# An early start, dummy matmuls, 64-column tiles and crossbar transposes in a fused attention and token-mixing kernel

## Chip, cores, metric

One core of one Trainium2 chip. The metric is the device time of one execution in microseconds (us). A run counts as slow when it is over 1.5% above the fastest of the same kernel; comparisons use the other (fast) runs. The profiler's span is some 1.8 us shorter than the time of the same run.

## The reference, cut to what matters

```python
# x: 8 x 8 x 512 x 64 (batch, head, token, d), state: 8 x 8 x 32 x 64
a     = softmax(x @ state.T / 8);  xread = a @ state      # 512 tokens read 32 slots
a2    = softmax(state @ x.T / 8);  sread = a2 @ x         # 32 slots read 512 tokens
y     = concat([xread, sread], tokens)                    # 8 x 544 x 512 (heads side by side)
mixed = ((y @ w_q) @ (y @ w_k).T / 8) @ y                 # no softmax: V = (y@w_k).T @ y is 64 x 512
out   = relu(mixed) @ w_out
```

## The kernel before

Per batch, with the names that the profile shows: `xT` transposes x on TensorE, `pt` forms the scores, `exp` their exponentials E, `rs`/`rinv`/`A` normalise on VectorE and GpSimd, `at` transposes A, `srd` and `sums` form the second read and its divisors, `wq`, `wk`, `g`, `v` build the 64 x 512 matrix V, `mix` applies it, `fin` multiplies by w_out (the largest item). The order of all steps on all engines is one list, ORDER; an entry is step, batch, engine (t TensorE, v VectorE, a ScalarE, p GpSimd). Each engine executes its entries in order. TensorE is PE below, VectorE DVE, ScalarE ACT, GpSimd POOL, the queue that issues loads and stores SP. A matmul is a weight load, which puts one operand into the array (the stationary one), and the matmul itself, which moves the other operand through it.

```python
nc.sync.dma_start(out=st_f, in_=state.rearrange("b h n d -> (b h) (n d)")...)   # all state, 512 KB, first
for g in range(4):                                     # x of batch 0, four transfers
    eng = nc.sync if g % 2 == 0 else nc.scalar
    eng.dma_start(out=x_f0[:, 2*g:2*g+2], in_=xsrc(0, 2*g, 2*g+2))
# ... 16 warm-up matmuls on zeros ...
def xT_mm(n, b, e):                                    # transposes on TensorE
    for q in range(NP):
        for u in range(2):
            nc.tensor.transpose(out=ps[:, u, q, :],
                in_=x_bf[b][:, NP*r+q, 128*u:128*u+128], identity=ident)
def pt_mm(n, b, e):                                    # 8 matmuls, 64 columns moved
    for u in range(2):
        for q in range(NP):
            nc.tensor.matmul(out=ps[:, 2*u:2*u+2, NS*q:NS*q+NS],
                lhsT=L[b][f"xTe{r}"][:, u, q, :], rhs=stT[:, b, :, NP*r+q, :], ...)
def fin_acc(ps, lhs):                                  # 4 matmuls, 512 columns moved
    for k in range(KC):
        nc.tensor.matmul(out=ps, lhsT=lhs(k), rhs=w_o[:, k, :], start=(k==0), stop=(k==KC-1))
# ... the other steps; loads of batches 1 to 7 on POOL ...
for tok in ORDER.split(): ...
```

The softmax here doesn't subtract the row's maximum and nothing guards it: scores larger than these inputs give would overflow.

## Time and profile before

| | before |
|---|---|
| median time | 96.12 us (95.58 to 96.66, 3 runs); 95.4 to 96.3 in later calls |
| span, profiled run | 93.4 us |
| busy: PE, DVE, ACT, POOL | 79.8, 56.2, 53.6, 44.6 us |
| instructions in PE's stream (two for each matmul) | 2,754 |
| first `mix` of batch 0; last matmul ends | 27.5 us; 87.75 us |

The prediction below shows the lines on which it rests. One view that it only quotes in words is this: busy time of each engine in a stretch (us busy and number of instructions; then the granted PE clock, the DMA share and GB/s; the DMA share is the time of all packets over that of 16 engines, and can go above 1, since packets' times can overlap), here from the first `mix` to the last matmul of the kernel before.

```profile
27.50:87.80 60.30, 59.07 (x908) 36.89 (x907) 40.15 (x71) 36.06 (x56) 26.43 (x30) 1.00 0.48 147
```

PE is busy for 59.07 of 60.30 us at full clock. That leaves 1.23 us.

### The profile page before, as it was taken

What the parts mean: (1) busy time and instruction counts of PE and PEld (TensorE: products, weight loads), DVE (VectorE), ACT (ScalarE), POOL (GpSimd) and SP (SyncE); (2) the same over time, 40 slices, a digit from 0 to 9 for tenths busy, and PEclk for the clock granted to TensorE, in tenths of its full rate; (3) what the DMA queues carried; (4) which work ended last, traced back from release to release, by engine and by line L of the source; (5) the groups of instructions that cost most, each with busy time, mean ns of one, the idle gap of its engine ahead of it and who ended that gap; (6) DMA issues with size and microseconds to landing.
All of it is one profiled execution on the core that took longest, in us unless ns stands there. A gap on an engine that the chain in (4) does not pass through costs nothing.

```text
span 93.4 us, 3134 instructions
## 1 busy us (share of the span) xinstructions
PE 79.8 (85%) x1376; PEld 53.4 (57%) x1376; DVE 56.2 (60%) x109; ACT 53.6 (57%) x80; POOL 44.6 (48%) x58
## 2 busy tenths in 40 slices
PE   5908098998995999999999999999999999999500
PEld 3506086896864676888366547646668644444100
DVE  1026948589584959896496198965786487222500
ACT  2324746687894687359967647864054876444200
POOL 7307994894499989899500009339750000000000
PEclk9998555599999999999999999999999999999985
DMA  1998799999999915500032517806455004428990
GB/s 28 305 260 193 94 160 156 205 203 194 197 199 197 201 18 232 225 11 0 0 130 102 225 22 213 311 30 270 186 225 232 0 0 164 173 39 300 400 363 21
DMA packets 12933, 15.13 MB, mean 162 GB/s; under 512 B 1592, under 2 KB 10296, under 8 KB 12856
## 3 DMA queue, kind: packets, MB, share of 16 engines
q0 software_dynamic: 7808, 4.19, 33.2%
q1 hardware_dynamic: 4280, 9.70, 29.3%
q10 hardware_dynamic: 832, 1.05, 3.8%
q8 instruction: 10, 0.16, 0.7%
q14 instruction: 3, 0.02, 0.1%
HBM read 10.22 MB, written 8.91 MB: 205 GB/s over the span
## 4 chain that ended last, share of the span: by engine, by line
PE 76%; ACT 6%; DMA 6%; DVE 4%; issue 2%; DVEq 0%
PE fin_ps L538 30%; PE xT_ps L246 9%; DMA st_f<-in_state_dram 6%; PE pt_ps L264 5%; PE mix_ps L504 5%; PE at_ps L322 4%; PE srd_ps L335 3%; PE wq_ps L398 3%; PE wk_ps L436 3%; DVE stT L139 3%; ACT xT L137 2%; PE fins_ps L538 2%; PE srd_ps L348 2%; PE v_ps L468 2%; PE g_ps L452 2%
## 5 line engine op out<-in xcount | busy, mean ns | idle before, releaser
L538 PE MATMUL fin_ps<-w_o,rmix 128*128 128x512 bf16 x128 | 30.0, 379 | 0.0
L309 POOL TENSOR_TENSOR A<-E,rinv 128x1024 bf16<-128x1024 bf16 (+1 forms) x9 | 15.3, 1718 | 15.5 <-DVE rinv L303 15.5
L538 PEld LDWEIGHTS <-rmix 128*128 128x128 bf16 x128 | 11.6, 98 | 12.5 <-ACT rmix L143 0.3
L137 ACT COPY ost<-fin_ps 128x1024 f32<-128x1024 f32 (+1 forms) x10 | 9.3, 928 | 14.1 <-PE fin_ps L538 13.6
L139 DVE COPY ost<-fin_ps 128x1024 f32<-128x1024 f32 (+1 forms) x8 | 8.7, 1089 | 11.1 <-PE fin_ps L538 7.5
L280 ACT ACTIVATE E<-pt_ps 128x512 bf16<-128x512 f32 x16 | 9.6, 603 | 4.3 <-PE pt_ps L264 4.3
L372 POOL TENSOR_TENSOR sbd<-srn,mask 128x256 bf16<-128x256 bf16 x16 | 9.5, 612 | 4.4 <-DVE srn L362 4.1
L295 DVE TENSOR_REDUCE rsum<-E 128x16 f32<-128x512 bf16 x16 | 10.6, 672 | 1.1 <-ACT E L280 1.1
L246 PE MATMUL xT_ps<-ident,x_bf 128*128 128x128 bf16 x128 | 11.0, 238 | 0.1
L145 DVE TENSOR_SCALAR rmix<-mix_ps 128x1024 bf16<-128x1024 f32 x7 | 8.5, 1223 | 2.7 <-PE mix_ps L504 2.6
L137 ACT COPY xT<-xT_ps 128x1024 bf16<-128x1024 bf16 x9 | 9.1, 1020 | 1.5 <-PE xT_ps L246 1.5
L143 ACT ACTIVATE rmix<-mix_ps 128x1024 bf16<-128x1024 f32 x9 | 9.3, 1032 | 0.7 <-PE mix_ps L504 0.5
L213 POOL TENSOR_TENSOR stbd<-st_bf,mask 128x256 bf16<-128x256 bf16 x16 | 9.3, 614 | 0.0
L246 PEld LDWEIGHTS <-x_bf 128*128 128x128 bf16 x128 | 8.4, 106 | 1.0 <-issue 0.4
L264 PE MATMUL pt_ps<-stT,xT 128*128 128x64 bf16 x128 | 7.1, 203 | 0.5 <-DVE xT L139 0.4
L504 PE MATMUL mix_ps<-wq,V 64*128 64x256 bf16 x64 | 5.7, 272 | 1.2 <-issue 1.1
...
L264 PEld LDWEIGHTS <-xT 128*128 128x128 bf16 x128 | 5.6, 105 | 1.6 <-DVE xT L139 0.5
L139 DVE COPY xT<-xT_ps 128x1024 bf16<-128x1024 bf16 x7 | 4.8, 686 | 2.2 <-PE xT_ps L246 2.0
L139 DVE COPY AT<-at_ps 128x1024 bf16<-128x1024 bf16 x7 | 4.8, 685 | 1.2 <-PE at_ps L322 1.2
L322 PE MATMUL at_ps<-ident,A 128*128 128x128 bf16 x64 | 5.0, 219 | 0.0
L504 PEld LDWEIGHTS <-V 64*128 64x128 bf16 x64 | 2.4, 94 | 3.8 <-issue 2.8
...
## 6 DMA issues: line engine op xcount, KB each, us to landing
...
```

The source lines that it names most:

```text
L137: nc.scalar.copy(out=out, in_=in_)
L139: nc.vector.tensor_copy(out=out, in_=in_)
L143: nc.scalar.activation(out=out, in_=in_, func=AF.Relu)
L213: nc.gpsimd.tensor_tensor(out=stbd[:, b, r], in0=st_bf[:, b, r : r + 1, :].to_broadcast((128, NP, D)), in1=mask[:, :, None].to_broadcast(( ...
L246: nc.tensor.transpose(out=ps[:, u, q, :], in_=x_bf[b][:, NP * r + q, 128 * u : 128 * u + 128], identity=ident,)
L264: nc.tensor.matmul(out=ps[:, 2 * u : 2 * u + 2, NS * q : NS * q + NS], lhsT=L[b][f"xTe{r}"][:, u, q, :], rhs=stT[:, b, :, NP * r + q, :], ...
L280: nc.scalar.activation(out=L[b]["E"][:, r].rearrange("p c q n -> p c (q n)"), in_=L[b][f"pt{r}"], func=AF.Exp, scale=float(scale),)
L295: nc.vector.reduce_sum(out=L[b]["rsum"][:, w], in_=L[b]["E"].rearrange("p r c q n -> p (r c q) n")[:, w], axis=AX.X,)
L309: eng.tensor_tensor(out=L[b]["A"].rearrange("p r c q n -> p (r c q) n")[:, w], in0=L[b]["E"].rearrange("p r c q n -> p (r c q) n")[:, w], ...
L372: nc.gpsimd.tensor_tensor(out=L[b]["sbd"][:, r], in0=L[b]["srn"][:, r : r + 1, :].to_broadcast((128, NP, D)), in1=mask[:, :, None].to_broa ...
L504: nc.tensor.matmul(out=ps[:, h, kk, :], lhsT=L[b]["V"][rows, 128 * k : 128 * k + 128], rhs=L[b]["wq"][rows, 0:SH], start=True, stop=True,)
L538: nc.tensor.matmul(out=ps, lhsT=lhs(k), rhs=w_o[:, k, :], start=(k == 0), stop=(k == KC - 1))
```

## The change

Five things, and a rewritten ORDER. The state is loaded with heads in rows and batch 0's part first, so that the transposes back go. Batch 1's x is asked for earlier. `fill` entries put 52 dummy matmuls on zeros into PE's waits, to keep its clock up. Entries marked `c` cut a matmul with 128 stationary columns into two with 64, meant to spare PE the change of tiling between neighbours. `xs` transposes x of batches 5 to 7 by a DMA through the crossbar.

```diff
-    nc.sync.dma_start(out=st_f, in_=state... # 512 KB)
+    def st_load(b0, b1):
+        nc.sync.dma_start(out=st_f[:, b0:b1], in_=st_src[:, 2 * b0 : 2 * b1])
+    st_load(0, 1)              # then x of batch 0, then st_load(1, 3); st_load(3, 8) behind a gate on POOL
+    def fill(n, b, e):
+        ps = psA.tile([128, 256], FP, name="fill_ps", tag="psA")
+        for w in range(b):
+            nc.tensor.matmul(out=ps, lhsT=zero[:, 0:128], rhs=zero, start=True, stop=True)
+    def mm(m, out, lhsT, rhs, **kw):
+        if m == "c":
+            for h in range(2):
+                lh = ... lhsT[:, 64 * h : 64 * h + 64]
+                nc.tensor.matmul(out=out[64 * h : 64 * h + 64], lhsT=lh, rhs=rhs, **kw)
+        else:
+            nc.tensor.matmul(out=out, lhsT=lhsT, rhs=rhs, **kw)
     def pt_mm(n, b, e):        # likewise xT, at, srT, wk, g, sums, fin, fs
-                nc.tensor.matmul(
+                mm(e,
+    def x_dT(n, b, e):
+        xT = work.tile([128, H, 2, 128], BF, name="xTd", bufs=3)
+        nc.sync.dma_start(out=xT..., in_=x_bf[b]..., transpose=True)
-    stb (state transposed back) and its copy, st_in (cast of the whole state)
 ORDER: rewritten; stores of fin are now entries of their own (os); the last tile is copied by halves
```

More of the change, by code (lines that the diff above doesn't have):

```diff
@@ L16 @@
 ORDER = """
-zst.0.p stc0.0.v stc1.0.a stt0.0.t xc0.0.p stt1.0.t xc1.0.a ste0.0.v ix1.0.p stf0.0.a xT0.0.t
-stf1.0.v ix2.0.p ste1.0.a iwo.0.p xc2.0.v stb.0.t xc3.0.v ix3.0.p xTe0.0.v stbe.0.a xT1.0.t wc.0.p
-pt0.0.t xTe1.0.v exp0.0.a pt1.0.t ix4.0.p rs0.0.v sw.0.t exp1.0.a sw.1.t rinv0.0.v xT0.1.t swe.0.a
-ix5.0.p rs1.0.v srd.0.t xTe0.1.a sums.0.t rinv1.0.v ix6.0.p sw.2.t srn.0.v xT1.1.t swe.2.a swe.1.v
-pt0.1.t A1.0.p srT.0.t xT1.2.t exp0.1.a srTe.0.v xTe1.1.v xT0.2.t xTe1.2.a A0.0.p at1.0.t rs0.1.v
@@ L22 @@
-pt1.1.t sw.3.t exp1.1.a xTe0.2.v pt1.2.t ix7.0.p at0.0.t swe.3.a srd.1.t ate.0.v pt0.2.t exp1.2.a
-stbd.0.p sums.1.t rs1.1.v wq.0.t exp0.2.a wks.0.t srn.1.v wk.0.t wqe.0.a sbd.0.p srd.2.t rinv.1.v
-wke.0.a srT.1.t xT1.3.t rs0.2.v srTe.1.a g.0.t sbd.1.p sums.2.t xTe1.3.a xT0.3.t ge.0.v srn.2.v
-v.0.t rs1.2.v xTe0.3.a sbd.2.p pt1.3.t srT.2.t srTe.2.v exp1.3.a ve.0.v pt0.3.t stbd.1.p xT1.4.t
-exp0.3.a rinv.2.v mixs.0.t mix0.0.t xTe1.4.v mse.0.a mix1.0.t A.2.p mxe0.0.a srd.3.t mxe1.0.v
-pt1.4.t sums.3.t xT1.5.t exp1.4.a xT0.4.t xTe1.5.v fin0.0.t A.1.p xTe0.4.a srn.3.v fin1.0.t rs1.3.v
@@ L28 @@
-rs0.3.v srT.3.t fin2.0.t sbd.3.p srTe.3.a rinv.3.v oe0.0.a at.1.t rs1.4.v pt0.4.t A.3.p at.2.t
-ate.1.a fin3.0.t ate.2.v exp0.4.a wq.1.t oe1.0.v wks.1.t stbd.2.p wqe.1.a wk.1.t srd.4.t wke.1.a
-wq.2.t rs0.4.v stbd.4.p wks.2.t g.1.t wqe.2.v wk.2.t sums.4.t wke.2.a ge.1.v at.3.t stbd.3.p srn.4.v
-g.2.t ate.3.v srT.4.t ge.2.a v.1.t srTe.4.a sbd.4.p rinv.4.v v.2.t ve.1.v wq.3.t ve.2.a wks.3.t
-wk.3.t wqe.3.v A.4.p mix0.1.t wke.3.v mixs.2.t mix1.1.t mxe0.1.a mixs.1.t mse.2.v pt1.5.t g.3.t
-mse.1.v xT1.6.t exp1.5.a stbd.6.p mix1.2.t xTe1.6.v xT0.7.t mxe1.1.a at.4.t rs1.5.v stbd.5.p pt1.6.t
@@ L34 @@
-ge.3.a fin2.1.t ate.4.v mxe1.2.a fin3.1.t stbd.7.p exp1.6.a mix0.2.t xTe0.7.a oe1.1.v v.3.t wq.4.t
-mxe0.2.a wks.4.t wqe.4.v pt0.7.t fin0.1.t ve.3.v exp0.7.a fin1.1.t rs1.6.v rs0.7.v mix0.3.t oe0.1.a
-mixs.3.t wk.4.t mse.3.v xT1.7.t wke.4.v fs.3.t mxe0.3.a fin2.2.t xTe1.7.a fin3.2.t fse.3.a g.4.t
-oe1.2.v pt1.7.t fin0.2.t exp1.7.a fin1.2.t ge.4.v rs1.7.v mix1.3.t oe0.2.a rinv.7.v v.4.t mxe1.3.v
-A.7.p srd.7.t ve.4.a sums.7.t xT0.6.t srn.7.v mix0.4.t xTe0.6.a mix1.4.t mxe0.4.v mixs.4.t sbd.7.p
-srT.7.t at.7.t mse.4.a pt0.6.t xT0.5.t exp0.6.a mxe1.4.v fin2.3.t xTe0.5.a fin3.3.t srTe.7.v ate.7.v
@@ L40 @@
-pt0.5.t oe1.3.a fin0.4.t rs0.6.v rinv.6.v fin1.4.t exp0.5.a A.6.p rs0.5.v srd.6.t oe0.4.a srd.5.t
-sums.5.t rinv.5.v fin0.3.t srn.5.v A.5.p fin1.3.t at.6.t oe0.3.v srT.5.t sums.6.t fin2.4.t sbd.5.p
-ate.6.v at.5.t fin3.4.t srTe.5.v srn.6.v wq.7.t ate.5.v oe1.4.a sbd.6.p wks.7.t srT.6.t wk.7.t
-wqe.7.v wq.5.t srTe.6.a wke.7.v wks.5.t wk.5.t wqe.5.v g.7.t wq.6.t wke.5.v ge.7.a wks.6.t wqe.6.a
-wk.6.t g.5.t wke.6.a v.7.t ge.5.v v.5.t ve.7.a g.6.t ve.5.a mix1.7.t ge.6.v mix0.7.t mxe1.7.a
-mixs.7.t v.6.t mxe0.7.v mixs.5.t mix1.5.t mse.5.a ve.6.a mse.7.v mix0.5.t fin2.7.1 mxe0.5.v mxe1.5.a
@@ L46 @@
-fin3.7.1 oc2.7.v mix0.6.t oc3.7.a mix1.6.t mixs.6.t fin1.7.1 mxe1.6.v mse.6.a mxe0.6.a fs.7.t
-oc1.7.v fin2.6.t fse.7.a fin3.6.t fin2.5.t oe1.6.a fin3.5.t fin0.5.t oe1.5.v fin1.5.t fin0.6.t
-oe0.5.a fin1.6.t fin0.7.1 oe0.6.v oc0.7.a
+zst.0.p ix1.0.p stc.0.v fill.2.t stt.0.c ste.0.a stbd.0.p stf.0.a xc1.0.a xc0.0.p xc2.0.v ix2.0.p
+fill.21.t xT0.0.c xc3.0.v xTe0.0.v fill.2.t xT1.0.c iwo.0.p stc.1.v fill.2.t pt0.0.c ix3.0.p
+xTe1.0.v fill.2.t stt.1.c exp0.0.a stf.1.v fill.2.t pt1.0.c ste.1.a ix4.0.p rs0.0.v exp1.0.a
@@ new lines @@
+rinv0.0.v stbd.2.p wc.0.a fill.9.t sums.0.c rs1.0.v fill.2.t srd.0.r fill.2.t xT0.1.t srn.0.v A0.0.p
+rinv1.0.v fill.2.t sw.0.r xTe0.1.v fill.2.t srT.0.c xT1.1.c A1.0.p at0.0.c srTe.0.v xTe1.1.a pt0.1.c
+swe.0.v stg.0.p at1.0.c ix5.0.p exp0.1.a pt1.1.c ate.0.v exp1.1.a xT0.2.c ix6.0.p rs0.1.v wq.0.c
+xTe0.2.a wks.0.c wk.0.c wqe.0.v xT1.2.c sbd.0.p rs1.1.v sums.1.c wke.0.a srd.1.r rinv.1.v g.0.c
+stbd.1.p pt0.2.c srn.1.v ge.0.a xTe1.2.v exp0.2.a fill.1.t v.0.c srT.1.c sbd.1.p ve.0.a pt1.2.c
+srTe.1.v rs0.2.v exp1.2.a fill.3.t mix0.0.r A.1.p mixs.0.r stc.2.v mix1.0.r mxe0.0.a sums.2.t
@@ new lines @@
+mxe1.0.v srd.2.r xT1.3.c mse.0.a stt.3.c xTe1.3.a stt.2.c rs1.2.v stbd.3.p fin2.0.c rinv.2.v stf.2.a
+stf.3.v xT0.4.c stbd.7.p ste.3.v xT1.4.c xTe0.4.a ste.2.v at.1.c fin3.0.c stbd.5.p ate.1.v xTe1.4.a
+pt1.3.c srn.2.v sw.1.r stbd.4.p oe1.0.a srT.2.c swe.1.v xT0.3.c wq.1.c xTe0.3.v A.2.p exp1.3.a
+os1.0.s sw.2.r sw.3.r swe.2.a rs1.3.v pt0.3.c wks.1.c wk.1.c exp0.3.a fin0.0.c wke.1.v stbd.6.p
+srTe.2.a rs0.3.v at.2.c swe.3.a pt0.4.c rinv.3.v fin1.0.c wqe.1.a sbd.2.p ate.2.v exp0.4.a g.1.c
+xs.5.s pt1.4.c oe0.0.a rs0.4.v sums.3.c A.3.p srd.3.r ge.1.v wq.2.c exp1.4.a srn.3.v wks.2.c wk.2.c
@@ new lines @@
+wqe.2.v srT.3.c wke.2.a v.1.c rs1.4.v sbd.3.p srTe.3.a at.3.c ve.1.a g.2.c ate.3.v sums.4.c srd.4.r
+ix7.0.p xs.6.s mixs.1.r ge.2.v mix1.1.r mse.1.a mix0.1.r srn.4.v mxe1.1.a v.2.c rinv.4.v sbd.4.p
+srT.4.c wq.3.c ve.2.v wks.3.c wk.3.c mxe0.1.a wqe.3.v pt1.5.c A.4.p mix0.2.r wke.3.v pt0.5.c
+exp1.5.a fin2.1.c srTe.4.v exp0.5.a rs1.5.v xs.7.s g.3.c mxe0.2.a fin3.1.c ge.3.v rs0.5.v v.3.c
+oe1.1.a rinv.5.v at.4.c ve.3.v A.5.p sums.5.c srd.5.r ate.4.v mix1.2.r mixs.3.r mix0.3.r mxe1.2.a
+os1.1.s mse.3.v pt0.6.c wq.4.c srn.5.v wks.4.c os0.0.s wk.4.c exp0.6.a wqe.4.v sbd.5.p srT.5.c
@@ new lines @@
+fin2.2.c srTe.5.v mxe0.3.a wke.4.v fin3.2.c rs0.6.v pt1.7.c oe1.2.a mix1.3.r pt0.7.c mxe1.3.v at.5.c
+exp0.7.a pt1.6.c os1.2.s fin0.1.c exp1.6.a ate.5.v fin2.3.c exp1.7.a rs0.7.v wq.5.c rs1.7.v wks.5.c
+fin3.3.c wqe.5.a rinv.7.v rs1.6.v A.7.p sums.6.c sums.7.c oe1.3.a srd.7.r rinv.6.v srd.6.r srn.7.v
+wk.5.c fin1.1.c os1.3.s srn.6.v wke.5.a A.6.p srT.7.c g.5.c srTe.7.v at.7.c ge.5.v fin0.3.c ate.7.v
+fin1.3.c sbd.6.p oe0.1.v at.6.c oe0.3.a sbd.7.p wq.7.c os0.1.s ate.6.v wks.7.c wk.7.c srT.6.c
+fin0.2.c wqe.7.v os0.3.s wke.7.a srTe.6.a g.7.c fin1.2.c ge.7.v v.7.c oe0.2.v wq.6.c ve.7.a wks.6.c
@@ new lines @@
+wk.6.c mixs.2.r wqe.6.a mix1.7.r os0.2.s mse.2.v mix0.7.r mxe1.7.a mixs.7.r wke.6.v g.4.c v.5.c
+ge.4.v g.6.c mse.7.v ve.5.a v.4.c ge.6.v fs.3.c mxe0.7.a ve.4.v mix1.5.r fse.3.v mixs.4.r mix1.4.r
+mxe1.5.a v.6.c mxe1.4.v fix1.7.c ve.6.a mix0.4.r mse.4.v oc1.7.a mixs.6.r mix1.6.r mxe0.4.v fix0.7.t
+mxe1.6.a mixs.5.r mix0.6.r mse.6.a mse.5.v mix0.5.r oc0.7.a mxe0.6.v fix2.7.t fs.7.t oc2.7.a
+mxe0.5.v fin0.6.t fse.7.v fin1.6.t fin0.4.t oe0.6.v fin1.4.t os0.6.s fin2.6.t oe0.4.v fin3.6.t
+os0.4.s fin2.4.t oe1.6.a fin3.4.t os1.6.s fin0.5.t oe1.4.v fin1.5.t os1.4.s fin2.5.t oe0.5.v
@@ L49 @@
+fin3.5.t os0.5.s fix3.7.t oe1.5.v oc3.7.b os1.5.s
 """
@@ L80 @@
     work = ctx.enter_context(tc.tile_pool(name="work", bufs=4))
-    tail = ctx.enter_context(tc.tile_pool(name="tail", bufs=6))
+    tail = ctx.enter_context(tc.tile_pool(name="tail", bufs=5))
     psA = ctx.enter_context(tc.tile_pool(name="psA", bufs=2, space=bass.MemoryType.PSUM))
@@ L85 @@
     x_bf = [const.tile([128, H, NC * D], BF, name=f"x_bf{b}") for b in range(B)]
-    st_f = const.tile([B * H, NS, D], FP, name="st_f")
-    st_in = const.tile([B * H, NS, D], BF, name="st_in")
+    st_f = const.tile([128, B, 2, D], FP, name="st_f")
     x_f0 = const.tile([128, H, NC * D], FP, name="x_f0")
@@ L100 @@
     zero = const.tile([128, 256], BF, name="zero")
+    gate = st_f[:, 3, 0, 0:1]
     rmix_s = const.tile([128, 2, KC, 4, NS], BF, name="rmix_s")
@@ L105, in xsrc @@
         return x[b, h0:h1].rearrange("h (p c) d -> p h (c d)", c=NC)
+    st_src = state.rearrange("b (r q) n d -> (q n) (b r) d", r=2)
     wsrc = [w.rearrange("(r q d) j -> r d q j", r=2, q=NP) for w in (moe_w_q, moe_w_k)]
     dst_x = out[:, 0:S].rearrange("b (p c) e -> b p c e", c=NC)
-    nc.sync.dma_start(
-        out=st_f, in_=state.rearrange("b h n d -> (b h) (n d)").rearrange("p (n d) -> p n d", n=NS)
-    )
+    def st_load(b0, b1):
+        nc.sync.dma_start(out=st_f[:, b0:b1], in_=st_src[:, 2 * b0 : 2 * b1])
+    st_load(0, 1)
     for g in range(4):
@@ L115 @@
         eng.dma_start(out=x_f0[:, 2 * g : 2 * g + 2], in_=xsrc(0, 2 * g, 2 * g + 2))
+    st_load(1, 3)
     for t in range(2):
@@ L145, in relu, with tr @@
             nc.vector.tensor_scalar(out=out, in0=in_, scalar1=0.0, scalar2=None, op0=ALU.max)
+    def fill(n, b, e):
[5 more added lines that the diff above has]
+            for h in range(2):
+                lh = lhsT[:, 2 * h : 2 * h + 2, :] if len(lhsT.shape) == 3 else lhsT[:, 64 * h : 64 * h + 64]
+                nc.tensor.matmul(out=out[64 * h : 64 * h + 64], lhsT=lh, rhs=rhs, **kw)
+        else:
+            nc.tensor.matmul(out=out, lhsT=lhsT, rhs=rhs, **kw)
+    def tr(m, out, in_):
+        for h in range(2):
+            w = slice(64 * h, 64 * h + 64)
+            if m == "c":
+                i = in_[:, 2 * h : 2 * h + 2, :] if len(in_.shape) == 3 else in_[:, w]
+                nc.tensor.transpose(out=out[w], in_=i, identity=ident)
+            elif m == "r":
+                nc.tensor.transpose(out=out[:, w], in_=in_[w], identity=ident[w, w])
+            elif h == 0:
+                nc.tensor.transpose(out=out, in_=in_, identity=ident)
     def load(n, b, e):
@@ L160, in x_cast, with st_gate, st_cast @@
             copy(e, o, i)
-    def st_cast(n, b, e):
-        w = slice(16 * int(n[-1]), 16 * int(n[-1]) + 16)
-        copy(e, st_in[:, w], st_f[:, w])
+    def st_gate(n, b, e):
+        nc.gpsimd.memset(gate, 0.0)
+        st_load(3, B)
+    SC = [(0, 1), (1, 3), (3, B)]
+    SG = [(0, 1), (1, 3), (3, 6), (6, B)]
+    def st_cast(n, g, e):
+        b0, b1 = SC[g]
+        copy(e, st_bf[:, b0:b1], st_f[:, b0:b1])
     def zeros(n, b, e):
@@ L173, in w_cast, with st_tr, st_ev @@
             copy(e, w_qk, w_f)
-    def st_tr(n, b, e):
-        g = int(n[-1])
-        ps = psB.tile([128, NS // 2, B * H], BF, name="stT_ps", tag="psB")
-        for m in range(NS // 2):
-            for c2 in range(2):
-                nc.tensor.transpose(
-                    out=ps[64 * c2 : 64 * c2 + 64, m, :],
-                    in_=st_in[:, g * (NS // 2) + m, :],
-                    identity=ident[0:64, 0:64],
-                )
+    def st_tr(n, g, e):
+        b0, b1 = SG[g]
+        ps = psB.tile([128, b1 - b0, 2, HN], BF, name="stT_ps", tag="psB")
+        for b in range(b0, b1):
+            for r in range(2):
+                for c2 in range(2):
+                    nc.tensor.transpose(
+                        out=ps[64 * c2 : 64 * c2 + 64, b - b0, r, :],
+                        in_=st_bf[:, b, r, :],
+                        identity=ident,
+                    )
         G[g] = ps
-    def st_ev(n, b, e):
-        g = int(n[-1])
-        c2 = 0 if n[:3] == "ste" else 1
+    def st_ev(n, g, e):
+        b0, b1 = SG[g]
+        c2 = 0 if n == "ste" else 1
         rows = slice(64 * c2, 64 * c2 + 64)
@@ L192, in st_ev @@
             e,
-            stT[rows, :, c2, :, g * (NS // 2) : (g + 1) * (NS // 2)],
-            G[g][rows].rearrange("p n (b h) -> p b h n", b=B),
-        )
-    def st_back(n, b, e):
-        ps = psB.tile([128, B, 2, D], BF, name="stb_ps", tag="psB")
-        for b in range(B):
-            for r in range(2):
-                nc.tensor.transpose(
-                    out=ps[:, b, r, :],
-                    in_=stT[0:64, b, 0, NP * r : NP * r + NP, :],
-                    identity=ident[0:64, 0:64],
-                )
-        G["stb"] = ps
-    def stb_ev(n, b, e):
-        copy(e, st_bf, G["stb"])
+            stT[rows, b0:b1, c2].rearrange("p b h n -> p b (h n)"),
+            G[g][rows].rearrange("p b r m -> p b (r m)"),
+        )
     def stbd_blk(n, b, e):
@@ L245, in xT_mm @@
             for u in range(2):
-                nc.tensor.transpose(
-                    out=ps[:, u, q, :],
-                    in_=x_bf[b][:, NP * r + q, 128 * u : 128 * u + 128],
-                    identity=ident,
-                )
+                tr(e, ps[:, u, q, :], x_bf[b][:, NP * r + q, 128 * u : 128 * u + 128])
         L[b][n] = ps
@@ L254, in xT_ev, with a_dT @@
         r = int(n[-1])
-        xT = work.tile([128, 2, NP, 128], BF, name=f"xT{r}")
+        xT = work.tile([128, 2, NP, 128], BF, name=f"xT{r}", bufs=3)
         copy(e, xT, L[b][f"xT{r}"])
         L[b][n] = xT
+    def x_dT(n, b, e):
+        xT = work.tile([128, H, 2, 128], BF, name="xTd", bufs=3)
+        nc.sync.dma_start(
+            out=xT.rearrange("p h u t -> p (h u) t"),
+            in_=x_bf[b].rearrange("p h f -> p (h f)"),
+            transpose=True,
+        )
+        for r in range(2):
+            L[b][f"xTe{r}"] = xT[:, NP * r : NP * r + NP].rearrange("p q u t -> p u q t")
+    def a_dT(n, b, e):
+        AT = work.tile([128, 2, NC, 128], BF, name="AT")
+        nc.sync.dma_start(
+            out=AT.rearrange("p r c t -> p (r c) t"),
+            in_=L[b]["A"].rearrange("p r c q n -> p (r c q n)"),
+            transpose=True,
+        )
+        L[b]["AT"] = AT
     def pt_mm(n, b, e):
@@ L263, in pt_mm @@
             for q in range(NP):
-                nc.tensor.matmul(
+                mm(
+                    e,
                     out=ps[:, 2 * u : 2 * u + 2, NS * q : NS * q + NS],
@@ L321, in at_mm @@
             for c in range(NC):
-                nc.tensor.transpose(
-                    out=L[b]["at"][:, r, c, :], in_=L[b]["A"][:, r, c, :, :], identity=ident
-                )
+                tr(e, L[b]["at"][:, r, c, :], L[b]["A"][:, r, c, :, :])
     def at_ev(n, b, e):
@@ L330, in srd @@
     def srd(n, b, e):
-        ps = psB.tile([128, 2, D + 1], FP, name="srd_ps", tag="psB")
         for r in range(2):
@@ L335, in srd @@
                     nc.tensor.matmul(
-                        out=ps[NS * q : NS * q + NS, r, 0:D],
+                        out=L[b]["srd"][NS * q : NS * q + NS, r, 0:D],
                         lhsT=L[b]["E"][:, r, c, q, :],
                         rhs=x_bf[b][:, NP * r + q, D * c : D * c + D],
-                        start=(r == 0 and c == 0),
-                        stop=False,
+                        start=False,
+                        stop=(r == 1 and c == NC - 1),
                         skip_group_check=True,
                     )
-        L[b]["srd"] = ps
     def sums(n, b, e):
+        L[b]["srd"] = psB.tile([128, 2, D + 1], FP, name="srd_ps", tag="psB")
         for r in range(2):
             for c in range(NC):
-                nc.tensor.matmul(
+                mm(
+                    e,
                     out=L[b]["srd"][:, r, D : D + 1],
@@ L351, in sums @@
                     rhs=ones,
-                    start=False,
-                    stop=(r == 1 and c == NC - 1),
+                    start=(r == 0 and c == 0),
+                    stop=False,
                     skip_group_check=True,
@@ L380, in srT_mm @@
         L[b]["srTp"] = psB.tile([128, HN], BF, name="srT_ps", tag="psB")
-        nc.tensor.transpose(out=L[b]["srTp"], in_=L[b]["srn"][:, :, :], identity=ident)
+        tr(e, L[b]["srTp"], L[b]["srn"].rearrange("p r d -> p (r d)"))
     def srT_ev(n, b, e):
@@ L435, in wk_mm @@
             for r in range(2):
-                nc.tensor.matmul(
+                mm(
+                    e,
                     out=L[b]["wkp"][:, c, :],
@@ L451, in g_mm @@
             for c in range(NC):
-                nc.tensor.matmul(
+                mm(
+                    e,
                     out=ps[:, r, :],
@@ L534, in mixs_ev, with fin_acc @@
         relu(e, rmix_s[:, b // 4, :, b % 4, :], L[b]["mixs"])
-    def fin_acc(ps, lhs):
+    def fin_acc(m, ps, lhs):
         for k in range(KC):
-            nc.tensor.matmul(
-                out=ps, lhsT=lhs(k), rhs=w_o[:, k, :], start=(k == 0), stop=(k == KC - 1)
+            mm(
+                m, out=ps, lhsT=lhs(k), rhs=w_o[:, k, :], start=(k == 0), stop=(k == KC - 1)
             )
@@ L543, in fin_mm @@
         c = int(n[-1])
-        if e == "1":
+        if n[:3] == "fix":
             ps = psB.tile([128, DM], FP, name="fin1_ps", tag="psB")
-            L[b][n] = ps
+            L[b][f"fin{c}"] = ps
         else:
@@ L551, in fin_mm, with fin_st @@
         t0 = 128 * (c % 2)
-        fin_acc(ps, lambda k: rmix[:, b, k, c // 2, t0 : t0 + 128])
+        fin_acc(e, ps, lambda k: rmix[:, b, k, c // 2, t0 : t0 + 128])
     def fin_ev(n, b, e):
         p = int(n[-1])
-        ost = work.tile([128, 2, DM], FP, name="ost")
-        copy(e, ost, L[b]["fin", p])
-        nc.sync.dma_start(out=dst_x[b, :, 2 * p : 2 * p + 2, :], in_=ost)
+        L[b]["ost", p] = work.tile([128, 2, DM], FP, name="ost")
+        copy(e, L[b]["ost", p], L[b]["fin", p])
+    def fin_st(n, b, e):
+        p = int(n[-1])
+        nc.sync.dma_start(out=dst_x[b, :, 2 * p : 2 * p + 2, :], in_=L[b]["ost", p])
     def fin_ev1(n, b, e):
@@ L562, in fin_ev1 @@
         ost = tail.tile([128, DM], FP, name="ost1")
-        copy(e, ost, L[b][f"fin{c}"])
-        (nc.scalar if e == "a" else nc.sync).dma_start(out=dst_x[b, :, c, :], in_=ost)
+        if e == "b":
+            for h, (f, eng) in enumerate((("v", nc.sync), ("a", nc.scalar))):
+                w = slice(h * DM // 2, (h + 1) * DM // 2)
+                copy(f, ost[:, w], L[b][f"fin{c}"][:, w])
+                eng.dma_start(out=dst_x[b, :, c, w], in_=ost[:, w])
+        else:
+            copy(e, ost, L[b][f"fin{c}"])
+            (nc.scalar if e == "a" else nc.sync).dma_start(out=dst_x[b, :, c, :], in_=ost)
     def fs_mm(n, b, e):
         ps = psB.tile([128, DM], FP, name="fins_ps", tag="psB")
-        fin_acc(ps, lambda k: rmix_s[:, b // 4, k].rearrange("p b n -> p (b n)"))
+        fin_acc(e, ps, lambda k: rmix_s[:, b // 4, k].rearrange("p b n -> p (b n)"))
         L[b]["fs"] = ps
@@ L579 @@
         "zst": zeros, "stt": st_tr, "ste": st_ev, "stf": st_ev,
-        "stb": st_back, "stbe": stb_ev, "stbd": stbd_blk,
-        "sw": sw_mm, "swe": sw_ev, "xT": xT_mm, "xTe": xT_ev, "pt": pt_mm, "exp": pt_exp,
+        "stg": st_gate, "stbd": stbd_blk, "fill": fill, "fix": fin_mm, "os": fin_st,
+        "sw": sw_mm, "swe": sw_ev, "xT": xT_mm, "xTe": xT_ev, "xs": x_dT, "as": a_dT, "pt": pt_mm, "exp": pt_exp,
         "rs": rs, "rinv": rv, "A": nrm, "at": at_mm, "ate": at_ev,
```

## The prediction

> **What bounds the kernel now.** I read the page's busy shares and slices first, then the chain that ended last in order of time, then TensorE's timeline. TensorE (PE) is busy 85% of the span, the next engine (VectorE, DVE) 60%, so the question is where PE is not at work and where it works at half clock. The slices, of 2.3 us each:
>
> ```profile
> PE   5908098998995999999999999999999999999500
> PEclk9998555599999999999999999999999999999985
> ```
>
> PE has gaps in the first 12 us, small ones to about 29 us, then none until the end; the granted clock is 0.5 from about 9 to 19 us. The chain says what the gaps wait for:
>
> ```profile
> 0.73 5.58 DMA st_f<-in_state_dram
> ...
> 7.89 1.22 DVE stT L139
> ...
> 10.40 1.01 ACT stT L137
> ...
> 14.24 0.61 PE pt_ps L264 x8
> ...
> 24.69 1.94 ACT xT L137 x2
> ...
> 28.07 1.08 issue
> ...
> 72.65 1.09 ACT V L490 x2
> ...
> 79.94 7.81 PE fin_ps L538 x36
> 87.75 0.02 issue
> 87.77 0.59 ACT ost L137
> ```
>
> Start, length, what. Until 14 us the chain is the whole state (512 KB, 5.6 us), its cast, 64 small transposes and 64-row copies in series. From 14 to 87.75 us it is nearly all PE, with waits of 0.32 us (at 22.6), 1.94, 1.08 and 2.2 (72.6 to 74.8). The last matmul ends at 87.75 and the span at 93.4, so 5.65 us are last copy and last store. The first matmul of mix0 for batch 0 starts at 27.5; from there to the last matmul are 60.3 us, of which the time slices of that stretch count PE busy 59.1, DVE 40.2, ScalarE (ACT) 36.1, GpSimd (POOL) 26.5. I cut the kernel at that instruction, as both kernels have it.
>
> **What a change of tile costs, and a 64-column pair.** PE's timeline (start, duration, line, stationary size):
>
> ```profile
> 34.82 1.03 PE L538 MATMUL fin_ps<-w_o,rmix 128*128 128x512 bf16 x4
> 35.78 0.41 PE L398 MATMUL wq_ps<-AT,sw 128*64 128x256 bf16 x4
> 36.02 0.28 PE L407 MATMUL wq_ps<-srT,w_qk 128*64 128x32 bf16 x8
> 36.14 0.29 PE L424 MATMUL wk_ps<-w_qk,srT 128*64 128x64 bf16 x8
> 36.37 0.41 PE L436 MATMUL wk_ps<-sw,AT 128*128 128x64 bf16 x8
> 36.71 0.42 PE L335 MATMUL srd_ps<-x_bf,E 128*32 128x64 bf16 x32
> ```
>
> Durations overlap, so I use start to start. Four fin matmuls normally take 0.86 us (32.83 to 33.69 in the same view); here 0.96, because wq has another stationary shape: a change costs 0.10. Wk to srd likewise: 0.34 against 0.24. From 36.02 to 36.37 eight pairs of 64-column matmuls took 0.35 including one change: 31 ns a pair, against 29 for one 128-column matmul of 64 columns moved (0.235 for 8). Pairs of 512 columns (v, 39.75 to 39.96) took 0.21, as one fin matmul does. So two 64-column halves run beside each other, and cost the same or slightly more.
>
> **What the Trainium skill says.** (1) "TensorEngine Tiling (Array Packing)", Tiling Modes, Key Properties: changing the tiling mode drains TensorE. The trace agrees, 0.10 us each. (2) Same page, Tile-to-Partition Mapping, Restrictions: column tiling disables Fast Weight Load. If that made weights slow, the pairs above would not run at 31 ns; the trace shows no such penalty. (3) "TensorE: Matmul & The Clock Gate", What's actually happening: half clock by default and after an idle window, full after about 3.4 us of sustained work. It agrees: the 16 warm-up matmuls of 256 columns took 3.60 us, 225 ns each, twice the 0.11 of later ones, and clock 0.5 follows the idle start. (4) "DMA: Bandwidth & Descriptors", Latency and other measured facts: a DMA transpose reached 261 GB/s in one kernel. No run here shows one. An estimate from that page: 512 KB at 261 GB/s is 2.0 us, plus some 2 us of latency (the trace's 256 KB stores land in 2.1): 4 us or more each.
>
> **The change part by part.**
> *State in head rows, early x1.* Batch 0's state is now 64 KB, first in the queue, so it should land about 2.5 us after its issue (256 KB transfers took 2.1 to 3.0 where nothing stood before them): 3.3 instead of 6.3. The state's transposes back and their 1.0 us copy go; batches 1-2 and 3-7 follow later. x0 (1 MB) no longer queues behind 512 KB, but the second batch's load now competes; I take x0 as complete at 7.
>
> *Dummy matmuls.* 52 of 256 columns at 0.107 are 5.6 us of PE. They are there to keep the clock and to lie in waits, but PE is in order, and each group between 64-column ones adds two changes. Before mix0 of batch 0 the new order holds: dummies 5.6; 25 changes, 2.5; six xT of 0.46, 2.8; six pt of 0.27, 1.6; the rest (state transposes, sums, srd, srT, at, sw, wq, wks, wk, g, v) 3.6. Sum about 16. The warm-up still ends at 4.65, so PE alone puts mix0 at 20.7, plus 0.8 for dummies before the clock rises. Walking the order with the old durations: xT0 after the 21 dummies at 8.0, its DVE copy (0.69) to 9.4, pt0 10.0, exp (0.60) to 11.0, pt1 11.5, srd at 13.8, wait for the second half of A on POOL (1.04) to 16.1, at 17.1, copy, wq 18.5, wk, g, v with their copies to 22.5. mix0 at **22.7** instead of 27.5: 4.8 us gained.
>
> *64-column tiles.* After mix0 the changes fall from 40 to 29 (counted in the two orders): -1.1 us. Against it, pt, wk and g each take 0.035 more (0.27 for 0.235): 24 groups, +0.8, and sums +0.2. Near zero.
>
> *x of three batches by DMA.* Six groups of 0.45 leave PE (2.7), and six copies of 0.69 to 1.02 leave DVE and ACT (5). But the old order had done nine xT before mix0, the new one six, so in the later stretch only 7 becomes 4: -1.35. The new order also still has two pt (+0.5), one srd with sums (+0.5), three sw (+0.4), two state groups (+0.6) to do.
>
> Sum for the later stretch: -1.1 +1.0 -1.35 +2.0 = +0.5. Adding up the old stretch from the durations gives 57.7, its measure without its 3.4 us of waits 56.9; so the new one has about 57.5 of work.
>
> *Waits left.* I give 2.0 to 2.5 in place of 3.4: fewer copies, but DVE still has about 48 us of work (its 56 less some 9 in the start) in 60.
> *Tail.* The last tile's copy is split over ACT and DVE, each half 0.35 instead of 0.59, with a smaller store: 4.9 instead of 5.65.
>
> Together: 22.7 + 57.5 + 2.3 + 4.9 = 87.4 of span. The old span of 93.4 belongs to a run of 95.16, its unprofiled median is 96.12; subtracting differences (4.8 start, 0.5 later stretch, 0.75 tail: 6.0) gives 90.1, adding the profiled run's own 1.8 to 87.4 gives 89.2. With part of the waits gone that the old start had, I say **88.5 us**, 8% less.
>
> **Rivals.**
> *A, the transpose takes over as the wait.* x of batch 7 is loaded only after sbd of batch 3 on POOL: 14 us of POOL work from about 18 us, so issued near 34, landed near 39, transposed at 43 to 46. Its first reader stands 24 us of PE work after mix0, at 47. For: all three transposes and the stores share one in-order queue, and if each takes 8 us rather than 4, the third is late. Against: batch 5's starts near 28 and is needed near 39. It would cost 3 to 5 us: 92 to 93.
> *B, the start gains more.* If the 0.8 us of cold dummies and the waits of my walk are not there, mix0 comes at 20.5 and all else follows: 86. For: nothing in the old profile says that the clock must stay low once PE is busy. Against: the dummies are a floor of their own.
> *C, DVE becomes the bound.* It would have 48 us in 60, with its order fixed. For: copies of PSUM tiles of 1.2 us hold their buffers. Against: in the old stretch it had 40 in 60 and PE waited 3.4. It would add 2 to 3: 91.
> *D, the 64-column form is slow in transposes or long runs.* At 10% on fin alone, 28 groups of 0.86, +2.4: 91.
>
> **Range and chances.** Without any wait PE needs 4.65 + 16 + 0.8 + 57.5 = 79 us; with 4.9 and 1.8 that is 85.7, a floor unless a duration is wrong. A or C alone gives 91 to 93. So 85.5 to 92.0. Slower by 2% would need a transpose over 10 us late or two rivals at once.
>
> **What would show it.** Right: mix0 of batch 0 near 22.7 with clock near 1.0 from 9 us on; 58 to 61 us from there to the last matmul; xT in 4 groups after it; pairs of 64 columns at 31 ns and fin at 0.86; no wait of PE on the transposes; last matmul to end below 5. Wrong: pt of batches 5 to 7 waiting for DMA (A); mix0 at 20 to 21 (B); waits for DVE copies above 4 us (C); fin groups above 0.9 (D). The whole is wrong if changes of shape do not cost the 0.10 each that I count.

## The result

| | before | changed |
|---|---|---|
| median time, first comparison | 96.31 us (4 runs) | 101.49 us (100.48 to 102.02, 4 runs) |
| ratio of fast runs, 95% interval | | 1.0513 [1.0404, 1.0623] |
| same, repeated (`after_again`) | 95.66 us | 100.04 us; 1.0455 [1.0415, 1.0496] |
| span | 93.4 | 98.1 |
| PE busy | 79.8 us | 82.6 us |
| instructions in PE's stream | 2,754 | 3,722 |
| first `mix` of batch 0 | 27.5 us | 25.2 us |

A ratio is the mean time of one kernel's fast runs over that of the other's of the same rounds, so it is not quite the ratio of the medians. The first profile of the changed kernel fell in a run counted as slow (102.02 us), so I took the profile again; every line below of the changed kernel is of that second profile, a fast run of 99.93 us.

The change made the kernel 5% **slower**; 88.5 us and a range of 85.5 to 92.0 had been predicted. The slices of PE and of its granted clock, changed kernel:

```profile
PE   5999998539769999496989499999999999999700
PEclk9999999985975999999999999999999999999996
```

The clock's low stretch of 9 to 19 us is gone, as intended. But PE, which had no gap after 29 us, now has several (slices marked 5, 3, 4, 6, 4), and the clock falls in some slices between 20 and 32 us. Its chain that ended last (the work that ended last, followed back to what each step waited for; start, length, what) names them:

```profile
17.31 0.22 PE wq_ps L435 x4
...
18.48 0.06 PE srd_ps L161 x5
18.55 2.56 issue
21.10 0.35 PE srd_ps L161 x11
...
25.30 0.33 PE mix_ps L543 x4
...
26.37 1.47 issue
...
40.28 1.47 issue
...
44.60 0.89 issue
...
51.01 0.40 issue
...
54.51 1.44 issue
```

"issue" is time in which the engine waited for nothing that the profile shows. These six are 8.23 us; the kernel before had two, 0.32 and 1.08. What is odd is their place. The first stands **inside** the sixteen matmuls of `sums`, after five of them, in the middle of a pair: the sixth reads the other half of the piece of E that the fifth reads, and writes the same tile. So no operand, buffer or engine that the profile shows can be what it waits for.

The stretches (PE, its weight loads, DVE, ACT, POOL, clock, DMA share, GB/s), changed kernel:

```profile
0.00:25.20 25.20, 21.18 (x454) 15.89 (x454) 12.63 (x34) 10.11 (x18) 18.75 (x29) 0.93 1.21 198
25.20:92.70 67.50, 61.44 (x1405) 41.08 (x1406) 44.75 (x84) 34.88 (x53) 25.41 (x30) 0.97 0.59 158
92.70:98.10 5.40, 0.00 (x0) 0.00 (x0) 0.68 (x2) 0.37 (x1) 0.00 (x0) 0.86 0.54 208
```

From the first `mix` to the last matmul it took 67.5 us, where the kernel before took 60.3: 2.4 us more work and 4.8 us more idle PE.

**What the odd waits have in common.** PE's stream, as built, can be numbered (a weight load and a matmul are one instruction each), and the matmuls of the trace counted along it. Every wait marked issue of over 0.25 us, in every kernel (best2 and start_only have none):

| kernel | number of the first instruction after the wait (length, us) |
|---|---|
| before | 704 (0.32), 960 (1.08) |
| changed, second profile | 704 (2.56), 958 (1.47), 1726 (1.47), 1982 (0.89), 2238 (0.40), 2494 (1.44) |
| changed, first profile (slow run) | 704 (2.44), 958 (1.90), 1726 (1.60), 2494 (1.62) |
| before64 | 960 (3.35), 1216 (1.72), 1982 (0.87) |
| noxbar | 704 (2.56), 958 (1.45), 1982 (0.37), 2238 (1.19) |
| nofill | 704 (3.01), 1726 (1.33), 1982 (2.08) |
| no64; fin64; no64_noxbar | 704 (1.15); 704 (1.66), 1728 (0.37); 704 (0.96) |
| no64_nofill; best1; split | 704 (0.40); 704 (1.28), 1212 (1.20); 704 (0.36), 1216 (0.26) |

All stand within four instructions of 192 + a multiple of 256 (704, 960, 1216, 1728, 1984, 2240, 2496), whatever operation happens to be there: `sums`, `srd`, `wq`, `wk`, `mix`, `g`, `at`, `fin`. And the page's queue lines show instructions as packets: before, ten of 16 KB, changed, fourteen.

```profile
q8 instruction: 10, 0.16, 0.7%
```

```profile
q8 instruction: 14, 0.23, 0.9%
```

The trace records when each of these packets moves. In the changed kernel's second profile the six that belong to the waits start at 18.67, 25.40, 39.36, 43.22, 49.12 and 53.54 us and take 0.93 to 0.97 us; PE goes on 1.33 to 1.48 us after the end of each. The first starts when PE already stands still. So the theory tested below, **theory F**: PE's instructions come in packets of 256 (16 KB for 256 is 64 bytes each), one fetch ahead, and where PE gets through 256 instructions faster than the next packet can come, it stands still. The Trainium skill knows these packets: "Runtime: NRT & Kernel Launch", Instruction fetch mechanics, says that an instruction memory is refilled in 16 KiB blocks of 256 instructions, the next fetched while the current one executes, and that the cost of crossing a boundary is "mostly hidden". The 256 agrees with the table; "mostly hidden" does not hold here: PE stood still for six of the changed kernel's fourteen packets, 8.23 us in all.

**What the half clock adds.** Clock records of the second profile show full clock from 4.4 to 96.6 us but for 21.50 to 24.92 and 28.33 to 31.74 us, each right after one of the first two long waits. PE is busy all through them at half speed:

```profile
21.10:24.90 3.80, 3.80 (x101) 2.97 (x102) 1.55 (x5) 1.46 (x4) 2.34 (x3) 0.55 1.37 186
28.40:31.70 3.30, 3.30 (x45) 2.30 (x42) 1.39 (x3) 1.80 (x2) 3.30 (x6) 0.50 0.07 11
```

That is 6.8 us at half clock, at most 3.4 us lost. That the waits cause it is not shown: two of the six were followed by it, four (of 0.40 to 1.47 us) were not.

### The profile page after: what moved, and what is told of

The parts are those of the page before. It is cut to its first block, busy times and chain, and to the rows that moved or that the text cites. A ratio compares the mean times of both kernels' runs of the same rounds, so it can differ in the third digit from the quotient of the medians.

```text
span 100.2 us, 4119 instructions
## 1 busy us (share of the span) xinstructions
PE 85.3 (85%) x1858; PEld 59.0 (59%) x1860; DVE 57.9 (58%) x118; ACT 45.5 (45%) x71; POOL 44.2 (44%) x58
## 3 DMA queue, kind: packets, MB, share of 16 engines
q10 hardware_dynamic: 1120, 1.44, 4.3%
## 4 chain that ended last, share of the span: by engine, by line
PE 80%; issue 9%; ACT 3%; DVE 2%; DVEq 1%; ACTq 0%
PE fin_ps L161 16%; PE fin_ps L163 11%; PE fill_ps L155 8%; PE pt_ps L161 5%; PE xT_ps L170 5%; PE mix_ps L543 4%; PE warm_ps L132 4%; PE at_ps L170 4%; PE srd_ps L371 3%; PE wk_ps L161 2%; PE g_ps L161 2%; PE v_ps L507 2%; PE srd_ps L161 2%; PE v_ps L516 2%; PE stT_ps L217 2%
## 5 line engine op out<-in xcount | busy, mean ns | idle before, releaser
L161 PE MATMUL fin_ps<-w_o,rmix 128*64 128x512 bf16 x136 | 17.9, 394 | 0.0
L142 ACT COPY ost<-fin_ps 128x1024 f32<-128x1024 f32 (+2 forms) x11 | 9.2, 839 | 19.0 <-PE fin_ps L161 7.0
L163 PE MATMUL fin_ps<-w_o,rmix 128*128 128x512 bf16 x58 | 13.4, 379 | 0.1
L163 PEld LDWEIGHTS <-rmix 128*128 128x128 bf16 x60 | 5.7, 98 | 7.0 <-issue 0.4
L161 PEld LDWEIGHTS <-rmix 128*64 128x64 bf16 x136 | 7.2, 115 | 4.2 <-issue 0.5
L155 PE MATMUL fill_ps<-zero 128*128 128x256 bf16 x52 | 9.3, 309 | 0.0
L142 ACT COPY xT<-xT_ps 128x1024 bf16<-128x1024 bf16 x5 | 5.0, 1012 | 7.9 <-PE xT_ps L170 7.9
L170 PE MATMUL xT_ps<-ident,x_bf 128*64 128x128 bf16 x144 | 6.5, 245 | 0.0
L170 PEld LDWEIGHTS <-x_bf 128*64 128x64 bf16 x144 | 5.4, 128 | 1.0 <-issue 0.9
L155 PEld LDWEIGHTS <-zero 128*128 128x128 bf16 x52 | 4.8, 109 | 1.7 <-issue 0.2
```

What stands on the lines that cost most here:

```text
L142: nc.scalar.copy(out=out, in_=in_)
L155: nc.tensor.matmul(out=ps, lhsT=zero[:, 0:128], rhs=zero, start=True, stop=True)
L161: nc.tensor.matmul(out=out[64 * h : 64 * h + 64], lhsT=lh, rhs=rhs, **kw)
L163: nc.tensor.matmul(out=out, lhsT=lhsT, rhs=rhs, **kw)
L170: nc.tensor.transpose(out=out[w], in_=i, identity=ident)
```

## The experiments

Twelve runs, all correct. The rivals: **P**, the pairs are as cheap as predicted and the loss lies in the transposes or the new order; **X**, the crossbar transposes cost by filling the DMA engines or the store queue; **N**, it is the number of instructions, not their rate; **D**, the 64-column form is slow in itself.

**1. no64: no pairs.**

```diff
-ORDER entries ending in .c
+the same entries ending in .t        # one 128-column matmul each
```

> The changed kernel with every 64-column pair put back to one 128-column matmul (2,666 instructions in TensorE's stream instead of 3,722; all else kept). Theory F (TensorE runs out of instructions: each stretch of 256 of its instructions comes in one 16 KB packet, and the four long waits marked issue, 7.6 us, stand exactly where a stretch ends): those waits fall below 2 us, the half-clock stretches after them go, time 90 to 94. Rival P (the pairs are as cheap as I predicted and the loss lies elsewhere, in the transposes or the order): some 12 more changes of shape at 0.10, time 100 to 103.

Measured: 94.42 us, ratio 0.9857 [0.98, 0.9914]. One wait of this kind is left, 1.15 us. This one letter turns a kernel 5% slower than before into one 1.4% faster (a difference below 2%). P is out for most of the loss. The time is 0.4 us above the range that F expected, and one half-clock stretch (26.64 to 30.06 us) is left, which F had said would go. Two other waits show in the trace: for the rest of the state and for the transpose of batch 7 (idle PE by what ended it: total, times, longest):

```profile
PE stT_ps L217 <- DVE st_bf L144: 1.9, 1, 1.9
PE srd_ps L371 <- issue: 1.1, 1, 1.1
...
PE pt_ps L163 <- DMA xTd<-x_bf: 0.9, 1, 0.9
```

**2. before64: the pairs alone, in the kernel before.**

```diff
-nc.tensor.matmul / nc.tensor.transpose in xT, pt, at, srT, wk, g, sums, fin, fs
+the two 64-column halves              # ORDER untouched
```

> The kernel before with the same operations cut into 64-column pairs and nothing else changed (4,066 instructions in TensorE's stream instead of 2,754). Theory F: waits marked issue grow from 1.4 us to 5 us or more, at every 256th instruction, half-clock stretches follow, time 100 to 105. Rival P: fewer changes of shape pay for the pairs, time 95 to 97.

Measured: 103.96 us, ratio 1.085 [1.0792, 1.0908]. The first wait, in PE's timeline of this run:

```profile
24.06 0.20 PE L429 MATMUL wk_ps<-w_qk,srT 128*64 128x64 bf16 x1
27.61 0.31 PE L429 MATMUL wk_ps<-w_qk,srT 128*64 128x64 bf16 x7 [3.35 <-issue]
```

The pairs alone cost 8.5%, with nothing else of the change present. After the first `mix` PE is as busy as before (59.8 us against 59.07), so the pairs' own work is nearly neutral, as predicted. What they cost is the waits (5.94 us of this kind, against 1.40) and the half clock: 20.5 us at half clock in the clock records before 40 us, against 10.2. The wait at 960 was 1.08 us in the kernel before and is 3.35 here, at other operations.

**3. noxbar: x of batches 5 to 7 by PE again, pairs kept.**

```diff
-xs.5.s  xs.6.s  xs.7.s
+xT1.5.c xTe1.5.a ... xT0.5.c xTe0.5.v ... (six groups and six copies, where places were free)
```

> The changed kernel with x of batches 5 to 7 transposed by TensorE again (in 64-column pairs; 192 more instructions, 2.7 us more TensorE work), copied by ACT and DVE. Theory F: the waits stay, perhaps shorter between 37 and 54 us where the transposes had filled the DMA engines; time 100 to 104. Rival X (the crossbar transposes are what costs, by filling the DMA engines or the store queue): the waits of 1.6 us at 42 and 56 us go and time falls to 96 to 98.

Measured: 101.83 us (fast runs 101.49 and 100.54). No gain from leaving the crossbar out, and the waits at 704 and 958 are the same (2.56, 1.45): X is out as the main cause (run 2 has no transposes and waits all the same). But its sign came true in part. The two waits that it said would go, at 1726 and 2494 (42 and 56 us in the first profile), are gone; those at 1982 and 2238 are now 0.37 and 1.19, and after 40 us the waits sum to 1.56 us where the changed kernel has 4.20. From 35 to 56 us the DMA share is 0.40 here and 0.86 there. So the transposes probably lengthen the later waits; the run can't isolate that, since it also gives PE six groups more and moves the stream against the packets. That the time gains nothing all the same fits what the transposes save elsewhere (run 7).

**4. nofill: no dummies, pairs kept.**

```diff
-fill.2.t  fill.21.t  fill.9.t ...      (13 entries, 52 matmuls)
```

> The changed kernel without the 52 dummy matmuls (104 instructions fewer). If the dummies earn what they cost: the clock is half from about 8 to 19 us, mix0 of batch 0 comes no earlier than 25, time 101 to 104. If they only cost (8 us of the chain that ended last): mix0 at 22, time 97 to 99. Theory F says nothing about them but that the waits marked issue stay, at shifted places.

Measured: 97.9 us; fast runs 97.25 and 97.05, ratio 1.0129 [1.0057, 1.0201]. The dummies cost 3 to 4 us. First `mix` at 23.1. The waits are there still, moved to other operations and standing at the same numbers (704, 1726, 1982): these belong to the stream, not to an operation.

```profile
PE g_ps L160 <- issue: 3.0, 1, 3.0
PE wk_ps L160 <- issue: 2.1, 1, 2.1
PE at_ps L169 <- issue: 1.3, 1, 1.3
```

**5. fin64: pairs in the long groups only.** As no64, but `fin` and `fs` keep their pairs.

> The changed kernel with 64-column pairs left in the fin and fs groups only (512 columns moved, long instructions) and the short ones (xT, pt, at, srT, wk, g, sums, state) whole again: 2,810 instructions in TensorE's stream, 144 more than with none, and more changes of shape. Theory F (only the number of instructions per time hurts): waits marked issue about as without pairs (3.6 us in all there), four fin pairs still 0.86 us, time 94.5 to 96.5. Rival D (the pair itself is slow): fin groups above 0.9 us, time above 97.

Measured: 95.43 us, ratio 0.9941 [0.9875, 1.0007]: 1.0 us above no64, with waits of 1.66 and 0.37 us. The `fin` matmuls take as long in both forms: in this run pairs start 216 ns apart (median), and so do the single matmuls of the last groups. So D is out; the extra time fits the extra changes of shape and somewhat longer waits, which one run can't divide.

**6. no64_nofill: neither pairs nor dummies.**

> Both undone: no 64-column pairs and no dummies. In the changed kernel leaving out the dummies took 4 us off. If that gain is the dummies' own time, it comes here too: 90.5 to 92.5. If it was only that the starved stretch ends moved elsewhere, or if the clock now goes to half in the first 20 us: 94 to 96.

Measured: 92.22 us (fast runs 91.70, 90.87; ratio 0.9506 [0.9407, 0.9606]). So without pairs, too, the dummies cost some 3 us. They put the first `mix` 0.5 us earlier (20.9 against 21.4), and lose it after:

```profile
20.90:87.80 66.90, 62.84 (x1009) 38.41 (x1008) 44.83 (x84) 35.10 (x53) 26.66 (x30) 0.97 0.68 171
```

```profile
21.40:84.40 63.00, 60.53 (x998) 37.56 (x1008) 44.88 (x84) 35.10 (x53) 26.70 (x30) 1.00 0.73 180
```

The first line is no64, the second no64_nofill. With dummies there is the longer wait at 704 (1.15, not 0.40), a longer wait for the state (1.94, not 0.97; the load is asked for 1.2 us later, at 14.95, since POOL's step before it waits for a score group behind the dummies), half clock from 26.64 to 30.06 and the wait for the transpose (0.86). That is read from the two profiles, not isolated further.

**7. no64_noxbar: no pairs, no crossbar.**

> No 64-column pairs, and x of batches 5 to 7 transposed by TensorE. If the crossbar transposes earn the 2.7 us of TensorE time that I counted: 95.5 to 97.5, against 94.4. If the wait for them (1.3 us without pairs) and their load on the DMA engines take that back: 93.5 to 95.

Measured: 98.3 us, ratio 1.0224 [1.0151, 1.0296]: 3.9 us above no64. The crossbar transposes are the part that pays. (The places of PE's transposes are mine, so some of the 3.9 may be theirs.)

**8. best1: no64_nofill with four moves in ORDER.**

```diff
-oc3.7.b os1.5.s      +os1.5.s oc3.7.b                  (last big store first)
-oc1.7.a ... mxe1.6.a +mxe1.6.a oc1.7.a                 (copy of mix before an output copy)
-A0.0.p A1.0.p stg.0.p +stg.0.p A0.0.p A1.0.p           (rest of the state earlier)
-sbd.3.p ix7.0.p      +ix7.0.p before A.2.p             (x of batch 7 earlier)
```

> No pairs, no dummies, and four moves in the order: the last 512 KB store ahead of the last half tile, the copy of mix 1 of batch 6 ahead of an output copy on ACT, the rest of the state and x of batch 7 asked for some 2 and 5 us earlier. Each wait that these moves remove was read off: 0.5, 1.1, up to 2 and 1.3 us. Expected 88.5 to 91; if earlier loads only slow the loads beside them, no better than without the moves.

Measured: 92.73 us; fast runs 91.35 and 91.11, ratio 0.9501 [0.9419, 0.9582]. A miss: no better than without the moves. The tail shrank from 5.5 to 5.1 us and the state landed at 21.5 instead of 23.7, but two waits for instructions came (1.28 at 704, 1.20 near 1212): PE, no longer held up by data, ran into the packet.

**9. after_again: the changed kernel once more.**

> The changed kernel once more, since its profile fell in a run counted as slow (102.02 us, the others 100.5 to 101.5). Theory F: the same four waits marked issue, at the same places of TensorE's stream (instructions 704, 958, 1726, 2494, 256 or a multiple apart), 6 to 8 us in all; time 100 to 102. If those waits belong to the slow run alone, they are gone or shorter by half here.

Measured: 100.04 us, ratio 1.0455 [1.0415, 1.0496], all four runs fast; six waits, 8.23 us. They are not a matter of the slow run.

**10. split: many more instructions, but long ones.** As no64_nofill, with

```diff
-mm(m, out=ps, lhsT=lhs(k), rhs=w_o[:, k, :], ...)              # 512 columns
+for n in range(4): mm(m, out=ps[:, 128*n:128*n+128], lhsT=lhs(k), rhs=w_o[:, k, 128*n:128*n+128], ...)
```

> No pairs and no dummies, but each fin and fs matmul of 512 columns cut into four of 128 (816 more instructions, 3,378 in all, near the 3,618 of the run without dummies that took 97 us). They all stand where the instructions are long. Theory F as a matter of rate (256 instructions must last longer than one fetch): no new waits marked issue, only the cut's own cost, four times 56 to 57 ns for 216, some 1.4 us in all: 92 to 94. Rival N (the number of instructions in the whole kernel costs, wherever they stand): 95 to 97.

Measured: 93.96 us, ratio 0.9791 [0.9743, 0.9839]; fast runs 93.34 to 93.97, 2.4 us above no64_nofill. The stream has 3,378 instructions, near nofill's 3,618, yet waits of this kind total 0.6 us where nofill has 6.4. After the first `mix` PE is busy 62.5 us (no64_nofill 60.5) and idle 2.3 (2.5), so most of the 2.4 us is the cut's own work; 1.4 had been expected. **The rate decides, not the number**, and N is out.

**11. best2: no64_nofill with only the two moves at the end.**

> No pairs, no dummies, and of the four moves only the two at the end (the last 512 KB store ahead of the last half tile; the copy of mix 1 of batch 6 ahead of an output copy on ACT), since the earlier loads had brought two waits of 1.2 us for instructions. 0.5 and 1.1 us less than without them: 90 to 91.5. If it equals the run without moves (91.3 in fast runs), the end is set by the stores and not by the order.

Measured: 92.45 us, one fast run of six (90.43); the rest count as slow. Inconclusive.

**12. start_only: no pairs, dummies or crossbar.** What is left: state in head rows, early x, the new order.

> No pairs, no dummies, no crossbar transposes: what is left of the change is the state in head rows, the early second batch and the new order. From the other runs by difference (91.3 in fast runs without pairs and dummies, 3.9 us more without the transposes when the dummies were in): 95.2, that is, no faster than before. If the early start is worth the 4.8 us that I predicted for it: 91 to 92.

Measured: 97.51 us, ratio 1.0206 [1.01, 1.0312]. The first `mix` comes at 19.9 us, 7.6 us before that of the kernel before, and the kernel is 2% slower. The early `mix` was bought with work put off: from there to the last matmul PE is busy 65.6 us in this run (59.1 in the kernel before) and idle 4.4 (1.2); it waits 2.8 us for the rest of the state and is at half clock from 25.4 to 28.8 us.

Adding the parts in turn, each on what stands before it, by the ratio to the kernel before: early start and order 1.021; with the crossbar 0.951; with the dummies 0.986; with the pairs 1.046 to 1.051.

## Why the prediction was wrong, point by point

- **"64-column tiles ... Near zero."** This step failed. Its terms were sound: pairs at 31 ns, `fin` at 0.86 us a group, PE as busy as before in before64. What it left out is that a pair is four instructions in place of two. In short groups 256 instructions then take 64 pairs of 31 ns, 2.0 us, against 128 matmuls of 29 ns, 3.7 us, before. After a wait ended (the second profile), the next packet started 1.05 us (27.84 to 28.89) to 4.3 us (21.10 to 25.40, during the loads of x) later; with 0.95 for the packet and 1.4 until PE goes on, a supply of 256 instructions takes an estimated 3.4 to 6.7 us. The old form lay at that limit, the new one beyond it. The kernel before's chain, quoted in the prediction, has "28.07 1.08 issue" in the middle of a `mix` group: the warning was there, and I counted it as a wait that would go away.
- **The dummies**, "5.6 us of PE", with 25 changes: that sum held roughly (24 changes in the trace; PE reached `wq` of batch 0 at 17.3 us, 18.5 predicted), as did that they would be a floor. That they cost 3 us on balance was not in it; I let them pay by the clock.
- **"mix0 at 22.7".** It came at 25.2. The one wait for instructions ahead of it is 2.56; half clock ran against a faster start.
- **"Waits left: 2.0 to 2.5".** Measured 6.1 us of idle PE in the later stretch, 5.67 of it waits for instructions. Rival A (the wait for the transpose) did not happen in the changed kernel, where each landed in 6.1 to 6.4 us and PE waited for none; once the pairs were gone it did, with 0.86 us. My estimate of 4 us each was too short.
- **"its measure without its 3.4 us of waits 56.9".** A second mistake, of bookkeeping: of the waits read off the chain, the 2.2 us at 72.6 were not idle PE; the chain merely went through ACT there. PE was busy 59.07, so the new stretch needed 59.6, not 57.5. Measured: 61.44, less at most 1.7 for the half clock in it, 59.7.
- **"x of three batches by DMA"** was undervalued: 3.9 us with dummies and 6.1 in fast runs without (no64_nofill against start_only), against 2.7 of PE time and copies that I gave no price.
- **The early start**, "4.8 us gained", is not worth that by itself (start_only: 2% slower).
- **Tail**: "4.9", measured 5.4. The half tile's store is issued ahead of the last 512 KB one.
- **The 88.5 itself** lies below both sums of the prediction, 90.1 and 89.2; the discount for "part of the waits" had no number behind it.

By size: the span was to be 87.4 and is 98.1. Waits for instructions are 8.2 of the difference and half clock up to 3.4; work undercounted by 2.2 and the tail by 0.5 are about balanced by other waits that did not come (1.9) and a start that was quicker than walked. Direct tests agree in size: taking the pairs out gains 5.6 us, putting them into the kernel before costs 8.

What stays open: why a packet's fetch starts when it does. It fits that it is asked for on entering the 256 before it and then waits behind other DMA traffic. The second profile, by packet:

| packet starts, us | 18.67 | 25.40 | 28.89 | 39.36 | 43.22 | 49.12 | 53.54 | 57.09 |
|---|---|---|---|---|---|---|---|---|
| us after PE began the 256 before it | 3.7 | 4.3 | 1.05 | 2.8 | 1.45 | 3.5 | 2.0 | 1.1 |
| DMA share in the us before the start | 1.45 | 1.45 | 0.31 | 1.23 | 1.33 | 1.21 | 1.16 | 0.16 |

The six with a share above 1 are the six with a wait. This is read from one profile and not without exception (in before64 a packet started 1.6 us after at a share of 0.0); no run set the load of the DMA engines apart.

## What to carry to other kernels

Count instructions as well as array time: where many short instructions follow each other, an engine can run out of them, and a rewrite that halves the work of each and doubles their number loses though every instruction is as fast as planned. Look for waits with no releaser in the middle of a group and number the stream: if they stand a fixed distance apart, fewer instructions there are the remedy that was tested here; less DMA traffic at those moments may be another and was not. And a milestone reached earlier says nothing if work was put off behind it; compare idle time of the binding engine, taken from its busy time and not from the chain.

## What the Trainium skill lacked or had wrong

- "Runtime: NRT & Kernel Launch", Instruction fetch mechanics: the blocks of 256 instructions agree, but crossing one is not "mostly hidden" where instructions are short. PE stood still for 0.3 to 3.35 us at such places, 8.2 us in the changed kernel (98.1 us of span) and 1.4 in the kernel before, and half-clock stretches of 3.4 us followed two of the waits. It lacks the condition: some 3.4 us (quiet) to 6.7 us (during loads) for 256 instructions, an estimate from the packets' times here, and that packets started later where the DMA engines were full (1.05 us against 4.3).
- "TensorEngine Tiling (Array Packing)", Performance Considerations, When to Use Tiling, lacks that column tiling doubles the instructions per unit of work: 8.5% slower in before64.
- "TensorEngine Tiling (Array Packing)", Tiling Modes, Key Properties: right that a change of mode drains; it lacks the size, 0.10 us each here.
- "DMA: Bandwidth & Descriptors", Latency and other measured facts: has a bandwidth for transposes of 261 GB/s. A crossbar transpose of 512 KB from SBUF to SBUF took 4.6 to 9.1 us from issue to landing in the runs here (6.1 to 6.4 in the changed kernel's second profile), its issue holding the queue for 1.8 to 5.7 us.
